# One x tile loaded later and multiplied last, and the narrow value products in one bank, in a fused joint-attention block

## Chip, core and metric

One core of a Trainium2 chip runs the whole program in one launch. The metric is the device time of one execution in microseconds: three runs of the kernel before gave 116.44, 116.47 and 116.78, so a median of 116.47 us. A change is called faster or slower here where it moves the time by more than 0.3%.

## What is computed

Two streams of tokens, image (2 batches of 256) and text (2 batches of 32), width D = 1152, go through one joint attention. Each stream is layer-normalised, scaled and shifted by columns that come from a conditioning vector `c`, projected to q, k and v with its own weights, and attends over both streams together; the result is projected, gated and added to the input.

```python
mod_i = (_silu(c) @ wmod_img).reshape(B, 6, 1, D)      # likewise mod_t
shi, sci, gai = mod_i[:, 0], mod_i[:, 1], mod_i[:, 2]
hi = _layernorm(x_img) * (1 + sci) + shi               # likewise ht
qkvi = hi @ wqkv_img                                   # likewise qkvt
q, k, v = concat([text, image], axis=1) of each third
p = _softmax(einsum('bqd,bkd->bqk', q, k) * D ** -0.5)
a = einsum('bqk,bkd->bqd', p, v)
out_i = x_img + gai * (ai @ wo_img)                    # likewise out_t
```

Everything is bf16 with float32 accumulation.

## The kernel before

The 512 image tokens are four tiles of 128 (`i` = 0 to 3; tiles 0 and 1 are batch 0, tiles 2 and 3 batch 1). The width is nine rows of 128 (`kt` = 0 to 8). The order of all instructions is written out by hand (`manual_schedule`): each engine works its own instructions in the order of the program text, and waits where an operand is not there yet.

**Loads.** All large loads go through SP's queue in the order of the text. At the head stand x tiles 0 and 1, the first scale columns (`load_sc(0)`), x tile 2, the first value chunk (`load_v(0)`), x tile 3 (L108), and then in turn scale columns and value rows by the chunks of `KC` (rows 0-1, 2-3, 4-5, 6-8), the last value chunk in two pieces (L113). The shift weight (`w_sh_i`, L117) follows in one transfer and the query weight (L118) in thirds; then come text, key, gate and output weights, each when one of six weight buffers is free.

**Front of the image stream.** Per tile, VectorE makes the statistics (`stats_of`, L162), ScalarE the root (`std_of`, L169), and VectorE the normalised tile `xn_i` (`out_of`, L174). TensorE transposes it in nine pieces (`x_transposes`, L187) into PSUM; ScalarE copies that into `hT_i`, some rows with the scale already in (`evac_scaled`, L192), the others plain (`evac_low`, `evac_high`). `mod_scale(ch)` makes the scale columns of a chunk on TensorE with two-column products (L204), VectorE or ScalarE adds one, and `apply_mod` multiplies the rows of `hT_i` that were copied plain, on VectorE (0), GpSimd (1) or ScalarE (2). With scaled but unshifted rows TensorE already works the value projection: `v_part(i, half, ch)` adds one chunk's products to one of seven open accumulators of 512 columns (L244), tile by half. A tile has 1152 value columns: two halves of 512 (`VW`) and 128 narrow ones (`NM` to `D`).

**Around the shift.** When seven accumulators are done, the eighth (tile 3, second half) is worked at L395. Then `rows_for_cols(w_sh_i)` makes the shift as rows in four strips (L368, L372), the narrow columns of tiles 2 and 3 follow in one bank (`v_rest`, L344), `select_cols` and `cols_out` turn the rows into columns (L384 to L391), and the narrow columns of tiles 0 and 1 cover that. Then 18 `apply_mod(..., True, ...)` add the shift to all of `hT_i` (the value's share of the shift is added as a constant at the end of attention). The image queries come next (`qk_img`, L445): three output rows at once over all `kt`, then one at a time; then strips for text, the keys, text projections, scores, softmax, attention and output.

**Banks.** PSUM is held by a pool of seven banks (`ps_mm`) and one small one (`ps_sm`). The transposes of a tile use one of each or two of the seven; `mod_scale` uses the small one, or one of the seven with `own=False`. Evacuations by `evac` go to VectorE and ScalarE in turn by a running index.

Of the kernel before, what the change touches and what calls it, by code (L numbers as in the profile page):

```python
# [14 lines left out]
def kernel(  # L15
# [89 lines left out]
    load_sc(0)  # L105
    load_x(2)
    load_v(0)
    load_x(3)  # L108
    for ch in range(1, len(KC)):
        load_sc(ch)  # L110
        if ch < len(KC) - 1:
            load_v(ch)
# [1 line left out]
        nc.sync.dma_start(w_v_i[:, k0:k1, :], w_view(wqkv_img)[:, k0:k1, 2 * D:3 * D])  # L114
    K3 = ((0, 3), (3, 6), (6, KT))
    K2 = ((0, 5), (5, KT))
    w_sh_i = load_w(wmod_img, 0)  # L117
    w_q_i = load_w(wqkv_img, 0, K3)  # L118


# [30 lines left out]
    def evac(out_ap, in_ap):  # L151
        if evac_idx[0] % 2 == 0:
            nc.vector.tensor_copy(out_ap, in_ap)  # L153
        else:
            nc.scalar.copy(out_ap, in_ap)  # L155
        evac_idx[0] += 1
# [16 lines left out]
        nc.vector.reciprocal(rstd[0:np_, :], rstd[0:np_, :])  # L173
        nc.vector.tensor_scalar(out_ap, x_ap, mv[0:np_, 0:1], rstd[0:np_, :], op0=ALU.subtract, op1=ALU.mult)  # L174

    xn_i = act.tile([P, NIT, D], bf, tag="A")
    hT_i = act.tile([P, KT, B * NI], bf, tag="Bt")

    mod_i = const.tile([P, 2 * KT, B], f32, name="mod_img")
# [55 lines left out]

    vacc = {}

    def v_part(i, half, ch):
        k0, k1 = KC[ch]
        if ch == 0:  # L240
# [5 lines left out]
        if k1 == KT:  # L246
            evac(v_i[:, i, half * VW:(half + 1) * VW], ps[:])


    def v_block(units, chs):  # L250
        for ch in chs:
            for (i, half) in units:
                v_part(i, half, ch)

    warm(4)
    silu_c()
# [26 lines left out]
    std_of(2)  # L283
    evac_high(0, tp0)
    evac_high(1, tp1)
    stats_of(3, 0, 1)
    out_of(2)
    v_block([(0, 0), (0, 1), (1, 0), (1, 1)], [0])
    evac_low(1, tp1, 2)
    tps = x_transposes(2, KT - 1)  # L290
    stats_of(3, 1, NCH)
    evac_scaled(2, tps, 2)
    std_of(3)
    mod_scale(1, "dve", own=False)
    for n, kt in enumerate(range(*KC[1])):
        apply_mod(kt, 0, 2, False, n)
    evac_low(2, tps, 2)
    evac_high(2, tps)
    v_block([(2, 0), (2, 1)], [0])
    out_of(3)  # L300
    for kt in range(*KC[1]):
        apply_mod(kt, 2, 3, False, 0)
    v_block([(0, 0), (0, 1)], [1])
    tps = x_transposes(3, KT - 1)
    evac_high(3, tps)
    evac_scaled(3, tps, 4)
    evac_low(3, tps, 4)
    v_block([(1, 0), (1, 1)], [1])
    mod_scale(2, "dve")
    for kt in range(*KC[2]):  # L310
        apply_mod(kt, 0, 2, False, 0)
        apply_mod(kt, 2, 4, False, 1)
    v_block([(2, 0), (2, 1)], [1])
    v_block([(3, 0)], [0, 1])
    v_i = act.tile([P, NIT, D], bf, tag="A")
    SEVEN = [(i, half) for i in range(NIT) for half in range(2)][:7]
    for (i, half) in SEVEN[:5]:
        v_part(i, half, 2)
    mod_scale(3, "dve")
    for b in range(B):  # L320
        for n, kt in enumerate(range(*KC[3])):
            apply_mod(kt, b * TPB, (b + 1) * TPB, False, (n + b) % 3)
    for (i, half) in SEVEN[5:]:
        v_part(i, half, 2)
    for (i, half) in SEVEN:
        v_part(i, half, 3)
# [13 lines left out]
    def v_rest(i0, i1):  # L340
        ps = ps_mm.tile([P, TPB, P], f32, tag="mm")
        for kt in range(KT):
            for i in range(i0, i1):
                nc.tensor.matmul(ps[:, i - i0, :], lhsT=hT_i[:, kt, i * P:(i + 1) * P], rhs=w_v_i[:, kt, NM:D],  # L344
                                 start=(kt == 0 and i == i0), stop=(kt == KT - 1 and i == i1 - 1))
        return ps

    def v_rest_out(i0, i1, ps):
        evac(v_i[:, i0:i1, NM:D], ps[:])

    NGG = 4
    RC = 2 * P
# [40 lines left out]
    ps = ps_mm.tile([P, VW], f32, tag="mm")  # L393
    for kt in range(KT):
        nc.tensor.matmul(ps[:], lhsT=hT_i[:, kt, 3 * P:4 * P], rhs=w_v_i[:, kt, VW:NM], start=(kt == 0), stop=(kt == KT - 1))  # L395
    evac(v_i[:, 3, VW:NM], ps[:])
    shr = rows_for_cols(w_sh_i, "shr")
    cps = ps_sm.tile([P, NCOL + B], f32, tag="sm")
    v_rest_out(TPB, NIT, v_rest(TPB, NIT))
    select_cols(shr, cps)  # L400
    cols_out(mod_i[:, 0:KT, :], cps, 0.0)
    vr = v_rest(0, TPB)
    SHE = ((0, 2), (0, 1), (2, 0), (0, 2), (1, 0), (2, 0), (0, 2), (1, 0), (2, 0))
    for kt in range(KT):
        for b in range(B):
            apply_mod(kt, b * TPB, (b + 1) * TPB, True, SHE[kt][b])
    v_rest_out(0, TPB, vr)
    nc.gpsimd.tensor_copy(shT32[:, :, 0:B], mod_i[:, 0:KT, :])

    w_sh_t = load_w(wmod_txt, 0)  # L410
# [432 lines left out]
```

## Time and profile before

| what | value |
|---|---|
| median of three runs | 116.47 us |
| span of the profiled execution, first to last instruction | 114.4 us |
| TensorE busy / VectorE / ScalarE / GpSimd | 109.5 / 53.3 / 34.3 / 27.9 us |
| granted TensorE clock | 1.000 |
| moved by DMA | 40.89 MB, mean 357 GB/s |
| 8 to 12 us: TensorE busy, DMA | 3.62 of 4 us, 343 GB/s |
| 16 to 20 us | 4.00 of 4 us, 388 GB/s |
| 24 to 28 us | 4.00 of 4 us, 410 GB/s |
| first query product | 31.61 us |

Times inside the execution count from its first instruction. A matmul's row in the trace lasts longer than its share of TensorE (a 512-column product 378 ns, with the next one starting 216 ns later), so a busy TensorE can still have waited; the weight loads' rows and the starts of the matmuls tell more. Of the 63 value products that the text has ahead of L395, the trace holds 60; the weight loads are all there, and three double steps in the starts are missing records, not waits. Landing means the time at which all parts of a transfer are in.

### The profile page before, as it was taken

How to read it: one execution, taken by the hardware profiler on the slowest of the kernel's cores; microseconds unless marked ns; L12 is line 12 of the kernel's file. 1: busy time of each engine (PE TensorE's matmuls, PEld its weight loads, DVE VectorE, ACT ScalarE, POOL GpSimd, SP SyncE). 2: the span in 40 equal slices, each digit the busy share in tenths (PEclk: the TensorE clock that was granted, in tenths of full speed). 3: DMA queues.
4: the chain of work that ended last, by engine and by line, in shares of the span. 5: the costliest groups of instructions: out<-in, count | busy, mean ns of one | idle time of the engine just before them, and what ended most of it. 6: DMA issues, size and time to landing. Idle time of an engine off the chain costs nothing.

```text
span 114.4 us, 2934 instructions
## 1 busy us (share of the span) xinstructions
PE 109.5 (96%) x1248; PEld 65.7 (57%) x1255; DVE 53.3 (47%) x137; ACT 34.3 (30%) x84; POOL 27.9 (24%) x59
## 2 busy tenths in 40 slices
PE   5998999999999999999999999999999999999990
PEld 1364564544944444486444546987687565667670
DVE  1699820452470402211832342136665803998571
ACT  2829660342370321021360122116555700001000
POOL 7000102540140000002224000001450560999100
PEclk9999999999999999999999999999999999999999
DMA  3999999999999999999999999999999999962142
GB/s 72 347 389 323 366 380 401 413 412 413 413 405 404 412 413 405 409 412 410 405 408 413 396 411 413 404 416 399 412 407 406 407 413 397 389 241 103 39 156 69
DMA packets 22744, 40.89 MB, mean 357 GB/s; under 512 B 1279, under 2 KB 6539, under 8 KB 22731
## 3 DMA queue, kind: packets, MB, share of 16 engines
q1 hardware_dynamic: 21648, 39.64, 90.8%
q0 software_dynamic: 608, 0.88, 2.1%
q10 hardware_dynamic: 475, 0.18, 0.7%
q8 instruction: 10, 0.16, 0.5%
q14 instruction: 3, 0.02, 0.1%
HBM read 39.36 MB, written 1.34 MB: 356 GB/s over the span
## 4 chain that ended last, share of the span: by engine, by line
PE 87%; DMA 7%; SPq 3%; issue 1%; DVE 0%
PE qkps L445 30%; PE ps L765 16%; PE va L244 10%; DMA w_sc_i<-in_wmod_img_dram 7%; PE aps L673 5%; PE ps L503 4%; PE sps L529 4%; PE gps L368 4%; PE ops L783 2%; PE ps L344 2%; SPq L93 2%; PE ps L395 2%; PE ps L604 2%; PE mps L204 1%; PE gps L738 1%; PE sps L542 1%
## 5 line engine op out<-in xcount | busy, mean ns | idle before, releaser
L445 PE MATMUL qkps<-hT_i,t 128*128 128x512 bf16 x158 | 35.4, 379 | 0.2
L445 PEld LDWEIGHTS <-t 128*128 128x128 bf16 x162 | 15.6, 98 | 18.3
L765 PE MATMUL ps<-t,aT 128*128 128x384 bf16 x99 | 16.4, 326 | 0.0
L765 PEld LDWEIGHTS <-aT 128*128 128x128 bf16 x117 | 11.0, 98 | 6.9 <-issue 0.5
L244 PE MATMUL va<-w_v_i,hT_i 128*128 128x512 bf16 x60 | 14.1, 378 | 0.2
L749 POOL TENSOR_TENSOR w_og<-t,gb 128x384 bf16<-128x384 bf16 x9 | 8.8, 1018 | 4.2 <-issue 4.2
L244 PEld LDWEIGHTS <-hT_i 128*128 128x128 bf16 x63 | 5.8, 97 | 6.5 <-POOL hT_i L228 0.5
L771 DVE TENSOR_TENSOR tmp<-ps,gb 128x384 bf16<-128x384 f32 x11 | 6.0, 549 | 6.1 <-DMA gb<-mod_scratch 4.4
L429 DVE TENSOR_SCALAR qkT<-qkps 128x512 bf16<-128x512 f32 x4 | 2.8, 692 | 11.6 <-PE qkps L445 11.6
L139 PE MATMUL wps<-wz 128*128 128x512 bf16 x16 | 6.3, 551 | 1.2 <-DVE wz L127 1.2
L162 DVE BATCH_NORM_STATS2 stats<-x_i 128x6 f32<-128x384 bf16 x12 | 5.9, 538 | 2.6 <-DMA x_i<-in_x_img_dram 2.6
L431 ACT ACTIVATE qkT<-qkps 128x512 bf16<-128x512 f32 x5 | 2.9, 596 | 13.5 <-PE qkps L445 13.5
L153 DVE CAST qkT<-qkps 128x512 bf16<-128x512 f32 x4 | 2.8, 692 | 7.7 <-PE qkps L445 7.7
L228 POOL TENSOR_SCALAR hT_i<-hT_i,mod_img 128x256 bf16<-128x256 bf16 x5 | 2.5, 514 | 15.6 <-DVE mod_img L213 12.3
L155 ACT CAST qkT<-qkps 128x512 bf16<-128x512 f32 x5 | 2.8, 587 | 10.6 <-PE qkps L445 10.6
L523 POOL COPY px<-pb 128x64 bf16<-128x64 bf16 x4 | 0.9, 238 | 19.8 <-DVE pb L521 19.8
L772 DVE TENSOR_TENSOR o<-tmp,x_i 128x384 bf16<-128x384 bf16 x11 | 5.4, 488 | 0.4
L456 POOL TENSOR_SCALAR svn<-svr 128x128 bf16<-128x128 bf16 x1 | 0.3, 300 | 20.6 <-DVE svr L153 20.6
L686 DVE TENSOR_SCALAR aT<-aps,sv 128x288 bf16<-128x288 f32 (+2 forms) x11 | 4.3, 456 | 2.0 <-PE aps L673 2.0
L503 PEld LDWEIGHTS <-t 128*128 128x128 bf16 x162 | 4.9, 98 | 0.2
L503 PE MATMUL ps<-hT_t,t 128*128 128x64 bf16 x162 | 4.9, 193 | 0.0
L673 PE MATMUL aps<-pT,v_i 128*128 128x288 bf16 (+2 forms) x44 | 4.8, 264 | 0.0
(159 smaller groups left out, 143.8 us busy)
## 6 DMA issues: line engine op xcount, KB each, us to landing
t<-in_wmod_txt_dram SPq DMA_DIRECT2D x3, 2592.0 KB, 21.5
t<-in_wmod_img_dram SPq DMA_DIRECT2D x2, 2592.0 KB, 22.3
t<-in_wqkv_img_dram SPq DMA_DIRECT2D x6, 864.0 KB, 13.6
t<-in_wqkv_txt_dram SPq DMA_DIRECT2D x2, 2592.0 KB, 17.2
t<-in_wqkv_txt_dram SPq DMA_DIRECT2D x3, 864.0 KB, 13.6
t<-in_wo_img_dram SPq DMA_DIRECT2D x1, 2592.0 KB
t<-in_wo_txt_dram SPq DMA_DIRECT2D x3, 864.0 KB, 15.5
w_v_i<-in_wqkv_img_dram SPq DMA_DIRECT2D x4, 576.0 KB, 8.2
```

Source lines behind the costliest of these rows:

```text
L139: nc.tensor.matmul(ps[:], lhsT=wz[:, 0:P], rhs=wz[:], start=True, stop=True)
L162: nc.vector.bn_stats(stats[0:np_, k, :], x_ap[:, k * CH:(k + 1) * CH])
L244: nc.tensor.matmul(ps[:], lhsT=hT_i[:, kt, i * P:(i + 1) * P], rhs=w_v_i[:, kt, half * VW:(half + 1) * VW], start=(kt == 0), stop=(kt == K ...
L368: nc.tensor.matmul(gps[32 * g:32 * g + 32, 0:RC], lhsT=lhs[:, kt, :], rhs=wt[:, kt, g * RC:(g + 1) * RC], start=(kt == 0), stop=(kt == KT ...
L445: nc.tensor.matmul(pss[j - j0][:], lhsT=wq[:, kt, j * P:(j + 1) * P], rhs=hT_i[:, kt, :], start=(kt == 0), stop=(kt == KT - 1))
L503: nc.tensor.matmul(ps[:, j - j0, :], lhsT=wq[:, kt, j * P:(j + 1) * P], rhs=hT_t[:, kt, :], start=(kt == 0), stop=(kt == KT - 1))
L529: nc.tensor.matmul(sps[:], lhsT=qkT[:, ft, b, q0:q0 + P], rhs=qkT[:, KT + ft, b, :], start=(ft == 0), stop=(ft == KT - 1))
L673: nc.tensor.matmul(bank[:, off:off + c1 - c0], lhsT=lhsT, rhs=rhs, start=(first[id(bank)] == n), stop=(final[id(bank)] == n))
L749: nc.gpsimd.tensor_mul(w_og[:, dt, 0:CH], w_o_i[:, dt, NG0:D], gb[:, B - 1, NG0:D])
L765: nc.tensor.matmul(ps[:, 0:cw], lhsT=aT[:, dt, t0:t0 + P], rhs=rhs, start=(dt == DTS[0]), stop=(dt == DTS[-1]))
L771: nc.vector.tensor_mul(tmp[:, 0:cw], ps[:, 0:cw], gb[:, b, cs])
L772: nc.vector.tensor_add(o[:, cs], tmp[:, 0:cw], x_i[:, i, cs])
```

## The change

In words: x tile 3 is loaded behind the third value chunk instead of behind the first. The shift weight is loaded in thirds. The second scale columns are made ahead of tile 2's transposes, and rows 2 and 3 of tiles 0 and 1 are scaled right after. Value products are issued in smaller steps (`v_wide`, `v_narrow`, `v_row`), and the narrow columns of all four tiles share one bank from the start, `vacc["n"]`, so that `v_rest` goes. Tile 3 is left out of the first rounds: its statistics come after the third scale columns, its transposes (`last_transposes`) after the last ones, and VectorE copies and scales them out in one multiply. Its first half and narrow columns are the last products ahead of the shift rows; its second half takes the place that `v_rest` had around `select_cols`. The image queries start with five output rows at once instead of three. `xn_i` shares its memory with the q and k tile instead of the value tile.

```diff
     load_v(0)
-    load_x(3)
     for ch in range(1, len(KC)):
+        if ch == len(KC) - 1:
+            load_x(3)
         load_sc(ch)
...
-    w_sh_i = load_w(wmod_img, 0)
+    w_sh_i = load_w(wmod_img, 0, K3)
...
-    xn_i = act.tile([P, NIT, D], bf, tag="A")
+    xn_i = act.tile([P, NIT, D], bf, tag="Q")
...
+    def v_wide(i, half, k0, k1, out=True):
+        if k0 == 0:
+            vacc[i, half] = ps_mm.tile([P, VW], f32, tag="mm", name=f"va{i}{half}")
+        ps = vacc[i, half]
         for kt in range(k0, k1):
             nc.tensor.matmul(ps[:], lhsT=hT_i[:, kt, i * P:(i + 1) * P], rhs=w_v_i[:, kt, half * VW:(half + 1) * VW],
                              start=(kt == 0), stop=(kt == KT - 1))
+        if k1 == KT and out:
+            v_wide_out(i, half)
+
+    def v_wide_out(i, half):
+        evac(v_i[:, i, half * VW:(half + 1) * VW], vacc[i, half][:])
+
+    def v_narrow(i, k0, k1):
+        if i == 0 and k0 == 0:
+            vacc["n"] = ps_mm.tile([P, NIT, P], f32, tag="mm", name="van")
+        for kt in range(k0, k1):
+            nc.tensor.matmul(vacc["n"][:, i, :], lhsT=hT_i[:, kt, i * P:(i + 1) * P], rhs=w_v_i[:, kt, NM:D],
+                             start=(i == 0 and kt == 0), stop=(i == NIT - 1 and kt == KT - 1))
+
+    def v_row(i, kt):
+        v_wide(i, 0, kt, kt + 1)
+        v_wide(i, 1, kt, kt + 1)
+
+    def last_transposes(k0, k1):
+        i = NIT - 1
+        b = i // TPB
+        tp = ps_sm.tile([P, k1 - k0, P], bf, tag="sm", name="tp")
+        for kt in range(k0, k1):
+            nc.tensor.transpose(tp[:, kt - k0, :], xn_i[:, i, kt * P:(kt + 1) * P], ident[:])
+        nc.vector.tensor_mul(hT_i[:, k0:k1, i * P:(i + 1) * P], tp[:],
+                             mod_i[:, KT + k0:KT + k1, b:b + 1].to_broadcast([P, k1 - k0, P]))
...
-    stats_of(3, 0, 1)
     out_of(2)
-    v_block([(0, 0), (0, 1), (1, 0), (1, 1)], [0])
     evac_low(1, tp1, 2)
+    for i in range(TPB):
+        for half in range(2):
+            v_wide(i, half, *KC[0])
+    mod_scale(1, "dve", own=False)
+    apply_mod(2, 0, 2, False, 0)
+    apply_mod(3, 0, 2, False, 1)
     tps = x_transposes(2, KT - 1)
-    stats_of(3, 1, NCH)
     evac_scaled(2, tps, 2)
...
+    evac_high(2, tps)
     evac_low(2, tps, 2)
...
+    for i in range(TPB):
+        v_narrow(i, *KC[0])
+    v_wide(2, 0, *KC[0])
     for kt in range(*KC[1]):
         apply_mod(kt, 2, 3, False, 0)
...
+    v_row(0, 2)
+    v_row(1, 2)
+    v_wide(2, 1, *KC[0])
+    v_narrow(2, *KC[0])
+    v_row(0, 3)
+    v_row(1, 3)
     mod_scale(2, "dve")
...
+    for i in range(TPB):
+        v_narrow(i, *KC[1])
+    for half in range(2):
+        v_wide(2, half, *KC[1])
+    v_narrow(2, *KC[1])
+    stats_of(3, 0, NCH)
+    std_of(3)
+    out_of(3)
     v_i = act.tile([P, NIT, D], bf, tag="A")
...
+    k0, k1 = KC[2]
+    for i in range(3):
+        v_row(i, k0)
+    for i in range(TPB):
+        v_row(i, k0 + 1)
+    v_row(2, k0 + 1)
     mod_scale(3, "dve")
...
+    for i in range(3):
+        v_narrow(i, k0, k1)
+    last_transposes(0, KT - 1)
+    k0 = KC[3][0]
+    for i in range(3):
+        v_row(i, k0)
+        v_narrow(i, k0, k0 + 1)
+    last_transposes(KT - 1, KT)
+    for i in range(3):
+        for half in range(2):
+            v_wide(i, half, k0 + 1, KT)
+        v_narrow(i, k0 + 1, KT)
+    v_wide(3, 0, 0, KT)
+    v_narrow(3, 0, KT)
...
     shr = rows_for_cols(w_sh_i, "shr")
     cps = ps_sm.tile([P, NCOL + B], f32, tag="sm")
-    v_rest_out(TPB, NIT, v_rest(TPB, NIT))
+    v_wide(3, 1, 0, 5)
     select_cols(shr, cps)
     cols_out(mod_i[:, 0:KT, :], cps, 0.0)
-    vr = v_rest(0, TPB)
+    v_wide(3, 1, 5, KT, out=False)
...
-    v_rest_out(0, TPB, vr)
+    v_wide_out(3, 1)
+    evac(v_i[:, :, NM:D], vacc["n"][:])
...
-    def qk_img(wq, blk, hooks):
+    def qk_img(wq, blk, jg, hooks):
...
-        groups = [(0, 3)] + [(j, j + 1) for j in range(3, KT)]
+        groups = [(0, jg)] + [(j, j + 1) for j in range(jg, KT)]
...
-    qk_img(w_q_i, 0, hooks={})
+    qk_img(w_q_i, 0, 5, hooks={})
...
-    qk_img(w_k_i, 1, hooks={0: txt_norm, 3: all_cols, 6: txt_transposes})
+    qk_img(w_k_i, 1, 3, hooks={0: txt_norm, 3: all_cols, 6: txt_transposes})
```

More of the change, by code (lines that the diff above doesn't have):

```diff
@@ L236 @@
     vacc = {}
-    def v_part(i, half, ch):
-        k0, k1 = KC[ch]
-        if ch == 0:
+    def v_wide(i, half, k0, k1, out=True):
+        if k0 == 0:
             vacc[i, half] = ps_mm.tile([P, VW], f32, tag="mm", name=f"va{i}{half}")
@@ L245, in v_part @@
                              start=(kt == 0), stop=(kt == KT - 1))
[L246 to L253, printed above, removed]
+        if k1 == KT and out:
[19 more added lines that the diff above has]
+                             mod_i[:, KT + k0:KT + k1, b:b + 1].to_broadcast([P, k1 - k0, P]))
     warm(4)
@@ L285 @@
     evac_high(1, tp1)
-    stats_of(3, 0, 1)
     out_of(2)
-    v_block([(0, 0), (0, 1), (1, 0), (1, 1)], [0])
     evac_low(1, tp1, 2)
+    for i in range(TPB):
[4 more added lines that the diff above has]
+    apply_mod(3, 0, 2, False, 1)
     tps = x_transposes(2, KT - 1)
-    stats_of(3, 1, NCH)
     evac_scaled(2, tps, 2)
[L293 to L296, printed above, removed]
+    evac_high(2, tps)
     evac_low(2, tps, 2)
-    evac_high(2, tps)
-    v_block([(2, 0), (2, 1)], [0])
-    out_of(3)
+    for i in range(TPB):
+        v_narrow(i, *KC[0])
+    v_wide(2, 0, *KC[0])
     for kt in range(*KC[1]):
         apply_mod(kt, 2, 3, False, 0)
[L303 to L308, printed above, removed]
+    v_row(0, 2)
[4 more added lines that the diff above has]
+    v_row(1, 3)
     mod_scale(2, "dve")
@@ L311 @@
         apply_mod(kt, 0, 2, False, 0)
-        apply_mod(kt, 2, 4, False, 1)
-    v_block([(2, 0), (2, 1)], [1])
-    v_block([(3, 0)], [0, 1])
-    v_i = act.tile([P, NIT, D], bf, tag="A")
-    SEVEN = [(i, half) for i in range(NIT) for half in range(2)][:7]
-    for (i, half) in SEVEN[:5]:
-        v_part(i, half, 2)
-    mod_scale(3, "dve")
[L320 to L326, printed above, removed]
+        apply_mod(kt, 2, 3, False, 1)
+    for i in range(TPB):
[6 more added lines that the diff above has]
+    out_of(3)
+    v_i = act.tile([P, NIT, D], bf, tag="A")
+    k0, k1 = KC[2]
[4 more added lines that the diff above has]
+    v_row(2, k0 + 1)
+    mod_scale(3, "dve")
+    for n, kt in enumerate(range(*KC[3])):
+        apply_mod(kt, 0, 2, False, (0, 1, 2)[n])
+        apply_mod(kt, 2, 3, False, (2, 0, 1)[n])
+    for i in range(3):
[12 more added lines that the diff above has]
+    v_narrow(3, 0, KT)
     for b in range(B):
@@ L338 @@
     pxs = [act.tile([P, 2, B, NT], bf, name=f"px_{q}") for q in range(TPB)] + [act.tile([P, 2, B, NT], bf, name="px_t")]
[L340 to L349, printed above, removed]
     NGG = 4
@@ L391, in cols_out @@
         nc.vector.tensor_scalar_add(dst[:, KT - 1, :], cps[:, NCOL:NCOL + B], add)
[L393 to L396, printed above, removed]
     shr = rows_for_cols(w_sh_i, "shr")
     cps = ps_sm.tile([P, NCOL + B], f32, tag="sm")
-    v_rest_out(TPB, NIT, v_rest(TPB, NIT))
+    v_wide(3, 1, 0, 5)
     select_cols(shr, cps)
     cols_out(mod_i[:, 0:KT, :], cps, 0.0)
-    vr = v_rest(0, TPB)
+    v_wide(3, 1, 5, KT, out=False)
     SHE = ((0, 2), (0, 1), (2, 0), (0, 2), (1, 0), (2, 0), (0, 2), (1, 0), (2, 0))
```

## The prediction

> **What bounds the kernel now.** I read the page first: how busy TensorE is, at what clock, and who sets the end.
>
> ```profile
> span 114.4 us, 2934 instructions
> PE 109.5 (96%) x1248; PEld 65.7 (57%) x1255; DVE 53.3 (47%) x137; ACT 34.3 (30%) x84; POOL 27.9 (24%) x59
> ...
> PEclk9999999999999999999999999999999999999999
> ...
> PE 87%; DMA 7%; SPq 3%; issue 1%; DVE 0%
> ```
>
> TensorE is the bound, at full granted clock. An edit that leaves its work alone can only win back its idle time. The chain of waits in order of time shows where that is left:
>
> ```profile
> 3.93 8.04 DMA w_sc_i<-in_wmod_img_dram
> 11.97 0.05 issue
> 12.01 0.61 PE mps L204 x18
> ...
> 14.48 0.50 PE tp L187 x9
> ...
> 20.19 0.65 PE mps L204 x27
> ...
> 26.28 1.94 PE ps L395 x9
> 28.22 0.03 issue
> 28.25 1.17 PE gps L368 x36
> ...
> 30.74 1.03 PE ps L344 x18
> ```
>
> The landing of the second scale columns at 11.97 is the last outside event on the chain; from 12.01 TensorE follows TensorE. The rows give prices: 0.216 us for a 512-column product (1.94/9), 0.057 for a 128-column one (1.03/18), 0.056 for a transpose, 0.024 to 0.025 for a two-column product. From 32.04 on the chain has nothing but matmuls at this pitch, so the change can matter only ahead of it. The weight loads' timeline (10 to 15 us, then 27.5 to 31.8 us) shows the waits:
>
> ```profile
> 11.26 0.51 PEld L187 LDWEIGHTS <-xn_i 128*128 128x128 bf16 x9 [0.76 <-DVE xn_i L174]
> 12.01 0.52 PEld L204 LDWEIGHTS <-w_sc_i 128*128 128x128 bf16 x18 [0.24 <-DMA w_sc_i<-in_wmod_img_dram]
> ```
>
> ```profile
> 28.25 0.89 PEld L368 LDWEIGHTS <-sT 128*32 128x32 bf16 x36 [0.52 <-DMA t<-in_wmod_img_dram]
> ```
>
> Eight wide products from 9.11 end at 10.84, so TensorE idles 0.43 us for the third tile's normalised rows, then 0.24 for the scale columns (nine transposes from 11.27 end at 11.77). The first value chunk costs some 0.1 near 13.4 (issued 4.54, 8.9 to landing). The shift weight costs 0.19: 26.12 plus nine products is 28.06, and L368 starts at 28.25. Together about 0.96 us.
>
> **The change, part by part.** *Work.* 18 narrow products of tiles 0 and 1 and 18 of tiles 2 and 3 become 36 into one bank; 72 wide ones, 36 transposes and 81 two-column products stay. TensorE's work changes by nothing; only order and waits do.
>
> *Tile 3's load.* It is issued behind the third value chunk, so what stood behind it lands earlier by its own transfer. The trace does not show that one apart. Lower bound: half of the 576 KB of value rows, which landed 1.46 us after x tile 2 (9.07 against 7.61), so 0.73. Upper bound: the scale columns landed 2.90 after that, and the next ones took 1.70, which leaves 1.20. I take 0.75, rows of the same length. Second scale columns: 11.97 - 0.75 = 11.2 (10.8 at the other end). The last scale columns have the same bytes ahead of them as before and stay at 10.78 + 8.9 = 19.7; the shift weight, at 28.2.
>
> *Second scale columns ahead of tile 2's transposes.* TensorE now idles from 10.84 to 11.25 for the columns: 18 products to 11.70, nine transposes to 12.20, four narrow products to 12.43. The next product needs ScalarE's scaled copy, which was the first transpose plus 0.65 (11.27 to 11.92) plus 0.37:
>
> ```profile
> 11.92 0.63 ACT L192 ACTIVATE hT_i<-tp,mod_img 128x128 bf16<-128x128 bf16 x2 [0.18 <-PE tp L187]
> ```
>
> So 12.77, a new idle of 0.34, and 0.05 more for the second of the two. Before, other products covered that copy; here four narrow ones do. Two wide products end at 13.25. Then six wide, two narrow, four wide: 15.52. Third scale columns (landed 15.1 before, 14.4 now) to 15.97; four narrow, four wide, two narrow, twelve wide: 19.76. The last scale columns have just landed at 19.7. Their 27 products end at 20.44.
>
> *Tile 3 at the end.* VectorE's statistics start when the third columns' scaling is out, near 16.9; x tile 3 lands about where the third value chunk did (7.28 + 9.3 = 16.6). Tile 2's chain on VectorE took 2.9 (8.33 to 11.21), so tile 3 is normalised at 19.8, ahead of need. Six narrow products end at 20.78; the transposes need the one small bank, freed as before some 1.03 after the 27 products begin: 20.79. Eight transposes to 21.24; six wide and three narrow cover the new scaling multiply for 1.46. Its price comes from the nearest multiply of a PSUM tile by a broadcast column:
>
> ```profile
> L490 DVE TENSOR_TENSOR hT_t<-tpt,mod_txt x2: 413/446/478, 65.4 to 65.8; 128x320 bf16<-128x320 f32 x1, 128x256 bf16<-128x256 f32 x1
> ```
>
> 65 ns for 64 columns: 1.19 us for 1024, from 21.5 to 22.7, and TensorE comes back for the bank at 22.70. Lower bound 0.7 (the 128x288 bf16 copy out of PSUM at L617 took 307 ns); upper bound 2.5, if stretched as L772 was (482 to 1016 ns) while GpSimd worked; I take 1.19, since L771, which also reads PSUM, kept 543 to 558 ns beside GpSimd. GpSimd is busy here too: its 0.57 us scaling stretched VectorE's next one from 0.29 to 0.51 at 21.28. SBUF — State Buffer of the Trainium skill, section "SBUF: two separate sides", says that VectorE with two SBUF inputs or in a two-port mode and GpSimd hold a shared port pair exclusively. By that rule the multiply, with one input in PSUM, keeps 1.19 and the sum stands, while the stretched L772 has two SBUF inputs; L771 agrees, and rival C below becomes less likely.
>
> Then one transpose, twelve wide, six narrow (25.7), nine wide and nine narrow for tile 3: 28.2.
>
> *Shift weight in thirds.* Only the last third can be waited for, from 28.2, and it is needed 6 x 0.11 = 0.65 after L368 starts. TensorE gets there at 28.2, so the 0.19 wait goes: covered either way. Two more issues on SP's queue at about 0.45 us hide behind transfers queued more than 10 us deep.
>
> *From L368 to the query products.* Before 3.36 us (28.25 to 31.61). After: 1.26 for the strips, five wide 1.08, selection 0.08, four wide 0.86: 3.28. But the first query product needs ScalarE's first shift:
>
> ```profile
> 31.01 1.31 ACT L230 ACTIVATE hT_i<-hT_i,mod_img 128x256 bf16<-128x256 bf16 x3
> ```
>
> The selection began at 30.55 and this shift, 0.51 long, ended at 31.52: 0.97 later. After: 28.2 + 1.26 + 1.08 + 0.97 + 0.05 = 31.56. Five accumulators need five of seven banks while two wait for evacuation: exactly free. They relax the shifts to one row per 1.08 us (0.65 before) and the query weight's thirds (30.4, 32.6, 34.7). The evacuations change engines by one in turn; 1.9 us between them hides that. The sum: 31.56 against 31.61, so -0.05, with one pipeline delay or another of 0.1 not counted. **I forecast no change: 116.5 us**, the median shown; the profiled span of 114.4 leaves 2.1 outside the first and last instruction, which the change does not touch.
>
> **Rivals.** *A, slower: the second scale columns land hardly earlier.* They head everything after 10.84 now, tile 2's transposes included, which before filled that wait. Each 0.1 us past 11.2 costs 0.1; from 11.6 it is over 0.35. At the old 11.97 it is 0.75: **117.2**. For: that landing was late against its neighbours (2.90 after the one before it, where 2.43 are due by 0.73 + 1.70), and a late packet stays late. Against: 288 KB really leave the queue ahead of it.
>
> *B, faster: columns land early.* At 10.8 the first idle of 0.41 goes and TensorE asks for the last scale columns at 19.35. If these stay at 19.7, 0.35 of it is given back and the gain is 0.1. But the page's queue of instruction loads (ten packets, 0.5% of 16 engines' span: 0.9 us each) held up one engine's share; with that packet elsewhere they land up to 0.5 earlier and the gain is 0.4: **116.1**. For: the table by stage has 343 GB/s from 8 to 12 us where 410 are reached later, so there is scatter. Against: both landings must be lucky. DMA: Bandwidth & Descriptors of the Trainium skill, section "Why a DMA increments its semaphore by 16 and not by 1", has each of up to 16 engines report by itself, so that the slowest decides; it speaks for either rival.
>
> *C, slower: the multiply is late.* It decides from 1.25 us; at 2.5 TensorE stands 1.3: **117.8**. Against: L771. *D: the change doesn't do what it says*, the query's five banks include one still held until the shifts are out, some 2 us: **118.5**. Against: no bank wait shows at 31.6 before, where the same two evacuations were pending.
>
> **How the numbers follow.** A measurement here cannot tell less than 0.3% (0.35 us) from no change. Forecast 0.50, its own range 116.15 to 116.85; A 0.20; B 0.20; C, D and smaller unseen waits 0.10. So faster 0.20, same 0.50, slower 0.30. Leaving out the tails of C and D: 116.05 to 117.2.
>
> **What would show it.** L204's second group at 11.2 to 11.3, ahead of tile 2's transposes; ScalarE as releaser of the first product of tile 2; the 27 products near 19.7; L368 near 28.2 without a DMA releaser; the query products near 31.6. It is wrong if the 27 products begin past 20.1, if a bank or VectorE releases TensorE after 20.8, or if the query products start over 0.35 off 31.6.

## The result and the profile after

The changed kernel took 117.27 us (median of 22 runs, 116.62 to 117.83) against 116.77 us for the kernel before in 22 runs beside it: a ratio of 1.0036, 95% interval 1.002 to 1.0051. That is slower by some 0.42 us (the medians alone are 0.50 apart), just past the 0.35 us that count as a difference here, and the interval reaches below them. The forecast was no change, 116.5 us. Taken from the 116.47 us that the forecast started from, the ratio gives 116.89 us: inside the whole range of 116.05 to 117.2, and 0.04 above the forecast's own range, which ended at 116.85.

The head of the page of the changed kernel, and the shares of its chain by engine:

```profile
span 115.2 us, 2939 instructions
...
PE 109.0 (95%) x1255; PEld 65.5 (57%) x1255; DVE 55.9 (48%) x139; ACT 32.2 (28%) x77; POOL 27.4 (24%) x59
...
PEclk9999999999999999999999999999999999999999
...
PE 90%; DMA 5%; SPq 1%; ACT 1%; issue 0%; DVE 0%
```

Nothing of size has moved: TensorE has the same work at the same clock and still sets the end. The span is 0.85 us longer than before, and the place of that has to be looked for in tenths of a microsecond. The chain of waits of the changed kernel in order of time (start, length, what) gives the front:

```profile
1.65 6.15 DMA w_sc_i<-in_wmod_img_dram
7.84 0.60 PE mps L205 x18
...
11.92 0.43 PE mps L205 x18
12.35 0.48 PE tp L188 x8
12.86 0.38 ACT hT_i L193
13.28 1.94 PE va L244 x8
...
20.44 0.66 PE mps L205 x27
...
28.86 1.10 PE gps L391 x36
...
32.23 17.57 PE qkps L465 x81
```

The landing that releases TensorE is now the first scale columns' (7.80); the second columns (L205) come ahead of tile 2's transposes (L188), and ScalarE's copy (L193) stands on the chain behind them. The weight loads' timeline of the changed kernel (start, length, what; idle time ahead and its releaser in brackets) has the waits:

```profile
11.72 0.54 PEld L205 LDWEIGHTS <-w_sc_i 128*128 128x128 bf16 x18 [0.29 <-DMA w_sc_i<-in_wmod_img_dram]
12.19 0.51 PEld L188 LDWEIGHTS <-xn_i 128*128 128x128 bf16 x9
...
13.28 0.10 PEld L244 LDWEIGHTS <-hT_i 128*128 128x128 bf16 x1 [0.35 <-ACT hT_i L193]
13.54 1.19 PEld L244 LDWEIGHTS <-hT_i 128*128 128x128 bf16 x7 [0.16 <-ACT hT_i L193]
...
20.06 0.94 PEld L205 LDWEIGHTS <-w_sc_i 128*128 128x128 bf16 x27
```

A bracket in these rows is idle time of the weight loads, which run ahead of the products. What TensorE itself loses is read from the starts of its products (9.5 to 13.6 us; the brackets in this view count from the modelled end of the product ahead):

```profile
10.04 1.89 PE L244 MATMUL va<-w_v_i,hT_i 128*128 128x512 bf16 x8 [0.35 <-ACT hT_i L193]
11.76 0.59 PE L205 MATMUL mps<-sT,w_sc_i 128*128 128x2 bf16 x18
12.21 0.66 PE L188 MATMUL tp<-ident,xn_i 128*128 128x128 bf16 x9
12.71 0.39 PE L256 MATMUL van<-w_v_i,hT_i 128*128 128x128 bf16 x4
13.28 0.65 PE L244 MATMUL va<-w_v_i,hT_i 128*128 128x512 bf16 x2 [0.18 <-ACT hT_i L193]
```

Eight products from 10.04, one every 0.216, end at 11.77, so TensorE loses nothing to the second columns. Four narrow ones from 12.71 end at 12.94 and the next product starts at 13.28: the copy costs 0.34, and 0.04 more at the product behind (13.54, which is 0.26 later). The weights of the last 27 scale products are loaded from 20.06 without a wait; the first of these products starts at 20.28. In the view of VectorE's multiply (duration shortest, median, longest in ns), the price that had been bounded only:

```profile
L269 DVE TENSOR_TENSOR hT_i<-tp,mod_img x2: 293/758/1224, 22.0 to 23.5; 128x1024 bf16<-128x1024 bf16 x1, 128x128 bf16<-128x128 bf16 x1
```

1.224 us for 1024 columns, while GpSimd was at work from 21.4 to 24.7.

Two places differ in the two profiles: the first query product starts at 32.16 (before: 31.61), and the stretch from the last matmul's start to the last instruction is 3.33 us (before: 2.97). Between these two, from the first query product to the last matmul's start, it is 79.75 (before: 79.81). The 0.36 at the end can be followed row by row. These are SyncE's semaphore waits on the program's last line (L838 before, L858 after; count, then duration in ns, then first and last start), asked for by half microseconds; a row that lies across a boundary stands on both sides of it. Before, from 112 to 113.5 us:

```profile
L838 SPq EVENT_SEMAPHORE  x2: 28/28/28, 112.4 to 112.4; - x2
...
L838 SPq EVENT_SEMAPHORE  x5: 28/28/28, 112.5 to 112.8; - x5
...
L838 SPq EVENT_SEMAPHORE  x2: 28/28/28, 113.2 to 113.5; - x2
```

After, from 112.5 to 114.5 us:

```profile
L858 SPq EVENT_SEMAPHORE  x1: 28/28/28, 112.9 to 112.9; - x1
...
L858 SPq EVENT_SEMAPHORE  x2: 28/28/28, 113.7 to 114.0; - x2
...
L858 SPq EVENT_SEMAPHORE  x7: 28/28/28, 114.0 to 114.3; - x7
```

The last matmul starts at 111.42 before and at 111.91 after. At the end SyncE waits in a fixed order for nine things: one, and then the eight semaphores on which the transfers issued by SP and ScalarE report that they are done. Before, seven of these waits are over by 112.8, while the last two output stores are still on their way; the eighth and ninth end with the stores, 1.79 and 2.05 us after the last matmul's start, and nothing is behind them. After, only the first is over by then. The second and third wait for the two stores (1.80 and 2.07), and six more stand behind them, one every 0.062 us: 6 x 0.062 = 0.37.

Why the order turned: the semaphores' numbers in the trace show that the transfers take the eight in turn. Before there are 48 transfers, and the last two stores get the seventh and eighth; the shift weight in thirds makes 50, and they get the first and second. SyncE's waits for the stores are longer, because the first of them begins before the other checks are made (us in total, times, longest; first before, then after):

```profile
SPq L838 <- DMA out_dram<-o: 0.6, 2, 0.4
```

```profile
SPq L858 <- DMA out_dram<-o: 1.0, 2, 0.8
```

### The profile page after: what moved, and what is told of

The parts are those of the page before. It is cut to its first block, busy times and chain, and to the rows that moved or that the text cites. A ratio compares the mean times of both kernels' runs of the same rounds, so it can differ in the third digit from the quotient of the medians.

```text
span 115.2 us, 2939 instructions
## 1 busy us (share of the span) xinstructions
PE 109.0 (95%) x1255; PEld 65.5 (57%) x1255; DVE 55.9 (48%) x139; ACT 32.2 (28%) x77; POOL 27.4 (24%) x59
## 4 chain that ended last, share of the span: by engine, by line
PE 90%; DMA 5%; SPq 1%; ACT 1%; issue 0%; DVE 0%
PE qkps L465 31%; PE ps L785 15%; PE va L244 14%; DMA w_sc_i<-in_wmod_img_dram 5%; PE aps L693 5%; PE ps L523 4%; PE sps L549 4%; PE gps L391 4%; PE ops L803 2%; PE mps L205 2%; PE ps L624 2%; PE van L256 2%; PE tp L188 1%; PE gps L758 1%; PE sps L562 1%; SPq L93 1%
## 5 line engine op out<-in xcount | busy, mean ns | idle before, releaser
L244 PE MATMUL va<-w_v_i,hT_i 128*128 128x512 bf16 x72 | 17.3, 379 | 0.5 <-ACT hT_i L193 0.5
L244 PEld LDWEIGHTS <-hT_i 128*128 128x128 bf16 x72 | 6.4, 98 | 6.4 <-ACT hT_i L193 1.0
L449 DVE TENSOR_SCALAR qkT<-qkps 128x512 bf16<-128x512 f32 x5 | 3.3, 688 | 12.7 <-PE qkps L465 12.7
L154 DVE CAST qkT<-qkps 128x512 bf16<-128x512 f32 x5 | 3.4, 690 | 7.7 <-PE qkps L465 7.7
L140 PE MATMUL wps<-wz 128*128 128x512 bf16 x16 | 5.6, 497 | 1.2 <-DVE wz L128 1.2
L229 POOL TENSOR_SCALAR hT_i<-hT_i,mod_img 128x128 bf16<-128x128 bf16 (+1 forms) x5 | 2.2, 447 | 16.1 <-DVE mod_img L214 16.1
L543 POOL COPY px<-pb 128x64 bf16<-128x64 bf16 x4 | 0.9, 236 | 19.8 <-DVE pb L541 19.8
L451 ACT ACTIVATE qkT<-qkps 128x512 bf16<-128x512 f32 x4 | 2.3, 596 | 11.6 <-PE qkps L465 11.6
L224 DVE TENSOR_SCALAR hT_i<-hT_i,mod_img 128x256 bf16<-128x256 bf16 (+1 forms) x16 | 4.3, 328 | 1.6 <-ACT hT_i L197 1.4
L156 ACT CAST qkT<-qkps 128x512 bf16<-128x512 f32 x4 | 2.3, 586 | 9.3 <-PE qkps L465 9.3
## 6 DMA issues: line engine op xcount, KB each, us to landing
t<-in_wmod_img_dram SPq DMA_DIRECT2D x3, 864.0 KB, 11.3
```

The costliest lines, as they stand in the source:

```text
L140: nc.tensor.matmul(ps[:], lhsT=wz[:, 0:P], rhs=wz[:], start=True, stop=True)
```

## The experiments

The expectations number their theories: 1, the wait for ScalarE's copy behind the second scale columns makes the change slower; 2, the new order of loads disturbs the early landings; 3, tile 3's late work and the queries do; 4, the order of the waits at the end does; 5, in the runs on counts, that the thirds cost at the front, and in the run on the columns, that the last scale columns' landing holds the front; 6, every transfer has a price at the end by itself. All are ratios to the kernel before on the same chip with 95% intervals. The times of the profiles come first, in us from the first instruction: the start of the weight loads for the first, second and last scale products, the first query product, and the end after the start of the last matmul. The scale products start with their weights where these came late, and up to 0.22 us behind them where TensorE was still busy.

| kernel | first | second | last | query | end |
|---|---|---|---|---|---|
| before | 6.93 | 12.01 | 19.81 | 31.61 | 2.97 |
| after | 7.84 | 11.72 | 20.06 | 32.16 | 3.33 |
| e1_tile2_first | 7.53 | 11.88 | 19.87 | 31.78 | 3.33 |
| e2_x3_early | 7.78 | 12.37 | 20.69 | 32.80 | 3.34 |
| e3_before_thirds | 7.46 | 12.34 | 20.12 | 31.80 | 3.33 |
| e4_one_shift_load | 7.50 | 11.37 | 20.02 | 31.95 | 2.97 |
| f1_thirds_same_count | 7.03 | 10.97 | 19.83 | 31.74 | 2.96 |
| f2_before_two_more | 7.58 | 12.21 | 20.32 | 32.22 | 3.32 |
| f3_tile2_first_one_load | 7.65 | 11.99 | 19.88 | 31.81 | 2.96 |
| f4_before_eight_more | 7.35 | 11.96 | 19.85 | 31.52 | 3.15 |
| g1_cols_ahead_of_x3 | 7.04 | 11.71 | 19.33 | 31.77 | 2.95 |
| e5_three_rows | 7.71 | 11.60 | 19.92 | 32.02 | 3.34 |
| h1_before_one_more | 7.92 | 12.54 | 20.44 | 32.11 | 3.39 |
| h2_before_one_less | 7.84 | 12.56 | 20.40 | 32.08 | 3.01 |

The first column is a warning. It follows the landing of the first scale columns, ahead of which no kernel here changes anything, and it lies anywhere from 6.93 to 7.92. A single profile's query product can therefore not be held against another's to better than some tenths; the end's column can.

**Tile 2's transposes first again.** The changed kernel, with the transposes ahead of the second scale columns as before:

```diff
-    mod_scale(1, "dve", own=False)
-    apply_mod(2, 0, 2, False, 0)
-    apply_mod(3, 0, 2, False, 1)
     tps = x_transposes(2, KT - 1)
     evac_scaled(2, tps, 2)
+    mod_scale(1, "dve", own=False)
+    apply_mod(2, 0, 2, False, 0)
+    apply_mod(3, 0, 2, False, 1)
```

> The changed kernel with one part undone: tile 2's transposes stand ahead of the second scale columns again, all else as changed. Theory 1 (the copy): the change loses by the new wait of some 0.4 us for ScalarE's copy of tile 2, which only four narrow products cover. Then the 18 column products cover that copy here, TensorE's step from the eighth value product to tile 2's first one shrinks from 1.5 to about 1.1 us, and the ratio to before falls from 1.0036 to 1.000 (-0.35 us against the changed kernel). If the last scale columns (19.7 to 20 us) then make it wait, half of that. Theory 2 (the load order): x tile 3 behind the third value chunk disturbs the first loads themselves, the order on TensorE is innocent: ratio stays at 1.003 to 1.004. Theory 3 (the end): the loss is in tile 3's late work (the multiply, the small bank) or at the query products: stays at 1.003 to 1.004 as well.

Measured: 1.0011 (0.9995 to 1.0028). By the starts of the products TensorE stands 0.17 us ahead of tile 2's first product (at 12.78), where the changed kernel has 0.34 and 0.04. Against that it stands 0.16 at 19.87, which the changed kernel doesn't; the weight loads' timeline of this kernel, whose idle time is longer than TensorE's, has the last scale columns as the releaser:

```profile
19.87 0.74 PEld L205 LDWEIGHTS <-w_sc_i 128*128 128x128 bf16 x27 [0.48 <-DMA w_sc_i<-in_wmod_img_dram]
```

Of the 0.21 that is won at tile 2's first products, 0.16 is lost at the last columns. The copy can't be read off as the cause from this run; the run of this order with one shift load, below, takes it away.

**x tile 3 loaded early again.** The changed kernel, with only the load's place undone:

```diff
     load_v(0)
+    load_x(3)
     for ch in range(1, len(KC)):
-        if ch == len(KC) - 1:
-            load_x(3)
         load_sc(ch)
```

> The changed kernel with only the load order undone: x tile 3 ahead of the second scale columns, all work as changed. Theory 1: the columns land some 0.75 us later and head all of TensorE's work, so it waits 0.4 to 0.75 longer for them; ratio to before 1.006 to 1.010, and the second group of column products starts near 12.0. Theory 2: the first loads recover, ratio 1.000 to 1.002. Theory 3: as theory 1 for the load, so 1.006 to 1.010.

Measured: 1.0089 (1.0068 to 1.011), the slowest of all. Its timeline of weight loads:

```profile
12.37 0.52 PEld L204 LDWEIGHTS <-w_sc_i 128*128 128x128 bf16 x18 [1.02 <-DMA w_sc_i<-in_wmod_img_dram]
```

That is 1.02 us of idle time of the weight loads ahead of the second columns. By the starts of the products TensorE itself stands 0.69 us there, and nothing with the late load, which is of the size of what separates the two ratios (0.0053, 0.62 us). So the load's move belongs to the new order of work and pays for it; the mechanism of rival A is real, but the late load keeps it away. Theory 2 falls.

**Only the thirds in the kernel before:**

```diff
-    w_sh_i = load_w(wmod_img, 0)
+    w_sh_i = load_w(wmod_img, 0, K3)
```

> The kernel before with one part of the change alone: the shift weight loaded in thirds. Theory 1 and 3: the 0.19 us wait ahead of the shift rows goes and nothing else moves: ratio 0.998 to 0.9985, L368 follows the last value product without a DMA as releaser. Rival: the wait stood in that one execution only, or comes back at the shift of the first row: 1.000. Theory 2 (more transfers disturb the queue): 1.000 to 1.002.

Measured: 1.0021 (1.0006 to 1.0036): slower with nothing of the front's order changed. The end grew to 3.33. The gain that was expected is 0.10 in the profile, not 0.19: TensorE stands 0.09 ahead of the shift rows here (28.44) without a transfer as releaser.

**The changed kernel with the shift weight in one load:**

```diff
-    w_sh_i = load_w(wmod_img, 0, K3)
+    w_sh_i = load_w(wmod_img, 0)
```

> The changed kernel with the shift weight in one transfer again. Theory 1 and 3: TensorE reaches the shift rows within 0.3 us of the weight's landing, so it loses 0 to 0.3 more: ratio to before 1.0036 to 1.006. Theory 2 as far as the thirds go: better than the changed kernel, 1.001 to 1.003.

Measured: 0.9989 (0.9971 to 1.0007), end 2.97. All the rest of the change is in this kernel, theory 3's work included, and it isn't slower than before. The two runs together point at the thirds; whether at their cost at the front (theory 5) or at the count (theory 4) is still open.

**The thirds kept, the count restored.** In the changed kernel the text's output weight, loaded in thirds far behind the front, is loaded in one:

```diff
-    w_o_t = load_w(wo_txt, 0, K3)
+    w_o_t = load_w(wo_txt, 0)
```

> The changed kernel, shift weight in thirds kept, with the text output weight in one transfer instead of three, so that the number of transfers issued by SP and ScalarE is 48 again as before, not 50. Theory 4 (the end): these transfers take eight completion semaphores in turn, and at the end SP checks the semaphores in a fixed order, some 62 ns each; with two transfers more the last two stores stand on the first semaphores checked, so the six other checks come behind their landing instead of ahead of it: +0.36 us from the last matmul to the end (2.97 to 3.33 in the traces so far). Then this kernel ends 2.97 us after its last matmul, and the ratio to before is 1.0036 - 0.0031 = 1.0005. Rival 5: the thirds cost at the front, by two more transfers among the first ones: the end may change but the ratio stays at 1.003 to 1.005.

Measured: 1.0018 (0.9998 to 1.0037), end 2.96. The end is back by 0.37 in the profile; the ratio moves by 0.0018 only, and its interval holds both theories' values.

**Two more transfers in the kernel before, the front untouched:**

```diff
-    w_o_t = load_w(wo_txt, 0, K3)
+    w_o_t = load_w(wo_txt, 0, ((0, 2), (2, 4), (4, 6), (6, 8), (8, KT)))
```

> The kernel before, shift weight in one transfer, with the text output weight in five transfers instead of three (two more transfers near the end, nothing else). Theory 4: 3.33 us from the last matmul to the end, ratio 1.003. Rival 5: the front is untouched, ratio 1.000 and the end as before.

Measured: 1.0043 (1.0025 to 1.0062), end 3.32. Two more transfers of a weight that is used long after the front make the kernel before as slow as the changed one. SyncE's waits at the end, from 112.5 to 114.5 us:

```profile
L838 SPq EVENT_SEMAPHORE  x1: 28/28/28, 113.0 to 113.0; - x1
...
L838 SPq EVENT_SEMAPHORE  x1: 28/28/28, 113.8 to 113.8; - x1
...
L838 SPq EVENT_SEMAPHORE  x7: 28/28/28, 114.1 to 114.4; - x7
```

The pattern is that of the changed kernel: the stores first, then a queue of waits behind them. Theory 5's cost of the thirds at the front isn't needed for it.

**Both undone: transposes first and one shift load.** The first experiment with the edit of the fourth.

> The changed kernel with two parts undone: tile 2's transposes ahead of the second scale columns and the shift weight in one transfer. Theories 1 and 4 together: 1.0036 less 0.0031 for the end less up to 0.0025 for the copy's wait: 0.998 to 0.9985. If the last scale columns' landing (19.7 to 20.0 us) holds TensorE in both, the wait for the copy was hidden by it and this is as the changed kernel with one shift load: 0.999. Rival: TensorE waits for the whole shift weight (28.2 to 28.6) as before: 0.999 to 1.000.

Measured: 1.0011 (0.9994 to 1.0028), end 2.96. The order with the copy (0.9989) is no slower than the one without it, so theory 1 falls. A miss stands beside it: this kernel has an end 0.37 shorter than the first experiment's and the same ratio. Both intervals are some 0.0033 wide, more than the 0.0031 (0.36 of 116.8) that is looked for.

**Eight more transfers in the kernel before:**

```diff
-    w_o_t = load_w(wo_txt, 0, K3)
+    w_o_t = load_w(wo_txt, 0, [(k, k + 1) for k in range(KT)])
...
-    w_v_t = load_w(wqkv_txt, 2 * D, K3)
+    w_v_t = load_w(wqkv_txt, 2 * D, ((0, 2), (2, 4), (4, 6), (6, 8), (8, KT)))
```

> The kernel before with eight transfers more (text output weight in nine instead of three, text value weight in five instead of three). Theory 4 in its exact form: what counts is the place in the turn of eight, so the end is as before (2.97 us) and the ratio 1.000. Rival 6: each transfer more costs at the end by itself (0.18 us each by the thirds): 4.4 us from the last matmul to the end, ratio 1.012.

Measured: 0.9993 (0.9971 to 1.0014). Four times as many added transfers as in the experiment two above, and no cost: by theory 6 it would be the slowest. With 56 transfers the last two stores are on the seventh and eighth semaphore again. SyncE's waits are those of the kernel before:

```profile
SPq L838 <- DMA out_dram<-o: 0.6, 2, 0.4
```

Its end of 3.15 is longer by 0.18 all the same, but not there: SyncE's wait for the last store ends 2.06 after the last matmul's start (before: 2.07). Its last drain then starts at 2.83 instead of 2.44 and takes 115 ns instead of 7; why, is open.

**The last scale columns earlier.** An attempt at a faster kernel: the first experiment with the count restored, x tile 3 loaded only ahead of the last value piece, so behind the last scale columns too, and all nine transposes of tile 3 just ahead of tile 2's last products:

```diff
     for ch in range(1, len(KC)):
-        if ch == len(KC) - 1:
-            load_x(3)
         load_sc(ch)
...
     for k0, k1 in ((6, 7), (7, KT)):
+        if k0 == 7:
+            load_x(3)
...
-    last_transposes(0, KT - 1)
...
-    last_transposes(KT - 1, KT)
     for i in range(3):
+        if i == 2:
+            last_transposes()
```

> The changed kernel with tile 2's transposes first, 48 transfers again (text output weight in one), and x tile 3 loaded behind the last scale columns and the first of the last two value pieces; tile 3 is normalised and transposed later still, ahead of the last products of tile 2, in one bank of each pool, and ScalarE alone takes the six accumulators of tiles 0 to 2 out. Theory 5 (what holds the front): in the kernels with the new order TensorE waits for the last scale columns at 19.8 to 20.0 us, and that wait swallows what the order of the work wins or loses ahead of it (so the two runs with tile 2 first were no faster). Here these columns land some 0.7 us earlier, the 27 products start at 19.2 to 19.5 without a wait for a DMA, the shift rows near 28.0, the query products near 31.4, and the ratio to before is 0.997 to 0.999. Rival: the front is held by the first landings (scale columns 0, value chunk 0), and the last columns' wait is only slack: then the 27 products still start at 19.8 or later, or tile 3's later chain makes a wait of its own, and the ratio is 1.000 to 1.003.

Measured: 1.0015 (0.9994 to 1.0035). Its weight loads:

```profile
19.33 0.94 PEld L205 LDWEIGHTS <-w_sc_i 128*128 128x128 bf16 x27
20.20 0.34 PEld L256 LDWEIGHTS <-hT_i 128*128 128x128 bf16 x6
20.95 0.11 PEld L244 LDWEIGHTS <-hT_i 128*128 128x128 bf16 x2 [0.40 <-DVE hT_i L224]
```

The last 27 products start without a wait, at 19.55 against 19.87 and 19.88 in the two kernels above with this order (e1, f3). Counted from the second scale products it is 7.78 against 7.94 and 7.83, so the columns' landing held them by 0.05 to 0.16 us, and the rest is an earlier start of this execution. The value products behind them then wait 0.39 for VectorE's scaling of the rows, and the shift rows come at 28.39, as in e1, where 28.0 was expected. What was won at the columns is lost again there.

**The queries with three rows first.** The changed kernel; theory 3's other half:

```diff
-    qk_img(w_q_i, 0, 5, hooks={})
+    qk_img(w_q_i, 0, 3, hooks={})
```

> The changed kernel with three query rows at the start instead of five, one look. Theory: the five rows only relax the shifts and the weight's thirds; with three the first products take 0.65 us per row of the width as before, the last third of the query weight (35.2 us in the changed kernel, needed 3.9 us after the first query product at 32.2) makes no wait, and from the first to the last matmul it takes 79.75 to 79.85 us, as in all kernels so far; 3.33 us to the end. Rival: the shifts or the weight come late by some 0.3 us, and it takes over 80.0.

Measured, in one execution: 117.27 us, end 3.34; from the first query product to the last matmul's start 79.77 us, where five rows have 79.75. The five rows neither gain nor cost.

**One more and one less.** Two more counts, in the kernel before; the front is as it was:

```diff
-    w_o_t = load_w(wo_txt, 0, K3)
+    w_o_t = load_w(wo_txt, 0, ((0, 2), (2, 4), (4, 6), (6, KT)))
```

> The kernel before with the text output weight in four transfers instead of three, one look at the end. Theory 4: one step in the turn puts the last store on the first semaphore that SP checks, and the seven other checks come behind its landing: 2.97 + 7 x 0.062 = 3.40 us from the last matmul to the end, more than with two transfers more (3.33). Rival 6 (each transfer costs by itself): 3.15.

```diff
-    w_o_t = load_w(wo_txt, 0, K3)
+    w_o_t = load_w(wo_txt, 0, K2)
```

> The kernel before with the text output weight in two transfers instead of three, one look at the end. Theory 4: the last store stands on the last semaphore but one, and one check comes behind its landing: 2.97 + 0.06 = 3.03 us from the last matmul to the end. Rival 6: 2.79.

Measured, in one execution each: with one more, the last store is on the first semaphore and seven waits stand behind it: end 3.39, time 117.39 us beside 116.75. With one less it is on the seventh, with one wait behind: end 3.01, time 116.69 us. The ends by count of transfers:

| transfers | waits behind the last store | end, worked out (us) | end, measured (us) |
|---|---|---|---|
| 47 | 1 | 2.97 + 0.06 = 3.03 | 3.01 |
| 48 | 0 | 2.97 | 2.95 to 2.97 |
| 49 | 7 | 2.97 + 0.43 = 3.40 | 3.39 |
| 50 | 6 | 2.97 + 0.37 = 3.34 | 3.32 to 3.34 |
| 56 | 0 | 2.97 | 3.15 (0.18 of it behind the last store's wait) |

The count of transfers by eights sets the end; theory 4 holds, and theory 6 falls.

## Why the prediction was right or wrong

**The step that failed** is the one on the shift weight: "Two more issues on SP's queue at about 0.45 us hide behind transfers queued more than 10 us deep." The transfers do hide, but their number doesn't: it turns the order in which the stores meet the waits at the end, and costs 0.36. With it fails the sentence that from 32.04 on the chain has "nothing but matmuls at this pitch, so the change can matter only ahead of it". The tail behind the last matmul, 2.97 us inside the span, was given no price. What lies outside the first and last instruction was indeed not touched: 2.04 us in the profiled execution of the changed kernel (117.28 less 115.24), where 2.1 was named. The sum of the prediction with this term is -0.05 + 0.36 = 0.31 us, a ratio of 1.0027, which the measured interval (1.002 to 1.0051) holds.

That the time still lies in the whole range is luck: the range was drawn for early and late landings, and no term of it stood for the tail. A slower outcome had a chance of 0.30, for other reasons.

**How firm that is.** In the profiles the end's length follows the count in every kernel, but for the 0.18 of the one with 56. In the times it is coarser: the four timed kernels with 50 transfers and without the early load (the changed one, e1, e3, f2) have a mean ratio of 1.0028, the four changed ones with 48 (e4, f1, f3, g1) 1.0008. The difference, 0.0020 or 0.23 us, is of the right sign, and smaller than 0.36; single ratios have intervals of 0.0015 to 0.002 to each side, which allows either. The cleanest comparison is within the kernel before, where no work moves: 1.0021 and 1.0043 with 50 transfers (e3, f2), on average 1.0032 or 0.37 us, and 0.9993 with 56 (f4). What is left of the 0.42, some 0.06, can't be told from nothing.

**Signs of being wrong.** The prediction named three, and in this profile they are there. The 27 products begin at 20.28, past 20.1; the query products begin at 32.16, 0.56 off 31.6; and at 21.35 the small bank holds TensorE for 0.06. The first two are one delay: the second scale products begin at 11.76, 0.51 behind the 11.25 that was worked out, in an execution whose first scale columns landed at 7.80 instead of 6.89. From there to the query products only 0.09 is added.

**The front: no change, as forecast, but not by the terms of the sum.** The same four kernels with 48 transfers stand at 0.9989 to 1.0018 in spite of all that was moved. In the profiles the first query product starts at 31.52 to 32.22, on average 31.89, in the six kernels with the front of before (before, e3, f2, f4, h1, h2), and at 31.74 to 32.16, on average 31.97, in the four with the order of the change (after, e4, f1, e5). Two terms came out otherwise and made up for each other, which is luck. The idle time of 0.41 for the second columns is in none of these four by the starts of the products. And the waits that were to be won back were read from the profile with the earliest start of all: TensorE stands 0.43 for tile 2's rows and 0.24 for the columns in it, but 0.24 to 0.29 and 0 to 0.18 in the five other kernels with that front. The steps, by the starts of the products:

- *Second scale columns.* Predicted 11.2 to 11.3, ahead of the transposes. Found 11.76 after a first landing 0.9 late, and 11.00, 11.40 and 11.62 in the three other kernels with this order (f1, e4, e5); so 11.25 lies among them, 0.2 ahead of their mean, and scatter as large as the whole range that was given is to be expected of such a number.
- *ScalarE's copy.* A new idle of 0.34 was predicted and 0.05 behind it; 0.34 and 0.04 are found in each of the four kernels.
- *From the second columns to the last 27 products:* 8.51 predicted, 8.52 found (11.76 to 20.28).
- *The last scale columns as the next thing that is late.* This was rival B's brake. In f1, with the earliest second columns of all (11.00), TensorE stands 0.31 for it at 19.83; in e4 it stands 0.10 at 20.03. The weight loads' rows name the landing (their idle time is longer than TensorE's):

```profile
19.83 0.74 PEld L205 LDWEIGHTS <-w_sc_i 128*128 128x128 bf16 x27 [0.64 <-DMA w_sc_i<-in_wmod_img_dram]
```

```profile
20.02 0.74 PEld L205 LDWEIGHTS <-w_sc_i 128*128 128x128 bf16 x27 [0.43 <-DMA w_sc_i<-in_wmod_img_dram]
```

  Where the work ahead of this landing is early, the landing takes part of the gain back. In the changed kernel's own profile and in e5 TensorE doesn't wait for it, so it isn't what kept the front even there.
- *Tile 3's statistics and the multiply.* x tile 3 landed at 17.86 where 16.6 was predicted, and was normalised at 20.77 where 19.8 was; its transposes went out at 21.35 all the same, held only by the small bank for 0.06, so the slack held. The multiply took 1.224 us, 1.19 predicted, but ran from 21.99 to 23.21, and the next transpose starts at 23.27: nothing of its cover was left. Rival C is out. SBUF — State Buffer of the Trainium skill, section "SBUF: two separate sides", has VectorE and GpSimd exclude each other only where VectorE runs in a two-port mode or reads two SBUF inputs. This multiply, with an input in PSUM, took 1.224 us beside a busy GpSimd, close to the 1.19 that was worked out, which agrees.
- *Shift weight.* The strips (L391) start with no transfer as releaser, as predicted; 8.51 after the 27 products, where 8.44 was. Of the wait of 0.19 that was to go, 0.09 stays: TensorE stands that long ahead of the strips here too (28.79).
- *From the strips to the queries:* 3.37 found, 3.36 the shortest that was worked out (ScalarE's first shift). No wait for a bank shows, so rival D is out.

**Rivals.** A's mechanism, a late second landing at the head of everything, is what the early load brings (1.0089, 0.69 us of TensorE's time); the change itself avoids it. B's early landings happened in f1's profile, and 0.31 was given back where 0.35 was written. B's other ground, that a packet of the instruction loads held up the second columns, was a misreading: in the trace of the kernel before all ten packets start at 15.97 or later, and those columns landed at 11.97. The slower outcome came by a way that no rival named.

## What to carry to other kernels

Price the tail behind the last matmul as its own stage: see which waits are still to come once the last output store has landed, and how the number of transfers in the program sets their order. When an edit splits or joins a load anywhere, count the transfers; here a split costs up to 0.42 us by its number alone, and joining or splitting another load, off the path, takes it back. Read what TensorE loses from the starts of its products, not from the idle time of the weight loads, and take the waits that a change is to win from more than one profile where early landings scatter. When a reorder wins time ahead of a transfer that everything waits for, ask when that transfer lands before counting the win.

## What the hardware showed that was not expected

- The waits at the program's end are worked through in a fixed order, one each 0.062 us where nothing is outstanding. Each lasts 28 ns in the trace, and seven of them behind the last landing put the end at 3.39 us instead of 2.97.
- The landing of the first scale columns, behind transfers that are the same in all kernels, varies by 1.3 us between profiled executions (6.54 in f1 to 7.88 in h1). The first of the last 27 scale products still starts anywhere from 19.83 to 20.65 over all kernels but e2 and g1, which move x tile 3's load.
- SyncE's last drain, 7 ns in the kernel before, started 0.39 us later and took 115 ns in one execution (f4), whose end was 0.18 us longer behind the last store's wait.
